# Float32r transposes of the unrounded attention words, released by a one-column POOL memset

## The chip, the cores and the metric

The kernel runs on one core of one Trainium2 chip. The metric is the device time of one execution in microseconds (us), here the median of three runs. The core has five engines that work through their own instruction lists in order: PE (TensorE: matmuls and transposes, with its weight loads shown apart as PEld), DVE (VectorE), ACT (ScalarE), POOL (GpSimd) and SP (which issues the transfers). They wait for one another through semaphores.

## The reference

```python
q_pool = q.reshape(B, H, S // 2, 2, D).mean(axis=3)          # B=2, H=8, S=1152, D=64
scores = (1 / sqrt(D)) * matmul(q_pool, k.transpose(0, 1, 3, 2))
attn = exp(scores - max(scores)); attn = attn / (sum(attn) + 1e-09)
x = matmul(attn, v)                                          # then laid out as [1152, 512]
h = maximum(x @ w_in, 0); x = (s * h * h + b) @ w_out        # d_ff 2048
out = ((x @ w_a) * (x @ w_b)) @ w_out2                       # d_ff 1536
```

All of it is float32. The kernel gets float32 accuracy by splitting operands into a high and a low float32r part (names in h and l) and adding the products.

## The kernel before, in words

Two heads make a pair; there are eight pairs, and each is a **round** of nine **blocks** of 128 pooled query rows by 1152 keys: blocks 0 to 3 are head 0, block 4 holds the rest rows of both heads, and 5 to 8 are head 1. A block g goes through these steps, on the engines named:

- S01 and S2 (L404, L411, PE): scores into PSUM, 768 and 384 columns.
- M01, M2, C (L427, L430, L435, DVE): the row maximum.
- X2, X01 (L439, L446, ACT): exp into the SBUF tile e, with row sums.
- A (L453, POOL, one column): the sum of the row sums; R (L457, DVE): its reciprocal.
- N (L464, POOL, 128x1152): e times the reciprocal, in place. Block 0 of the whole kernel does it in two pieces, columns 512 to 1151 first.
- Ta, Tb, Tc (L481, PE): nine 128x128 transposes of e, of 4, 4 and 1 in three PSUM banks. Here e is the stationary operand, which a weight load brings in, and the identity is what moves through.
- ha to hc (L493, ACT): the high part of each piece out of PSUM; La to Lc (L499, DVE): the low part, which frees the bank.
- PV matmuls (L515, PE) with the tiles p2h, p2l, p3h, p3l.

Beside them POOL splits k and v and pools q for the next pair (kc, v, qp, L95, L98, L325), and splits the attention output (xa_h, xa_l). PE also transposes k (L349, already float32r, three at a time, sharing a bank with Tc) and the pooled q (L369, float32). The order of all steps on every engine is written out by hand in a table, SCHED; nothing is reordered at run time. Three buffers of e go round, four PSUM banks are shared by the transposes, S2 and PV. After attention (about 268 us) come the two MLPs, in which PE does nearly all.

The lines that matter here:

```python
nc.gpsimd.tensor_scalar(out=e[:, c], in0=e[:, c], scalar1=m[:, 6:7], scalar2=1.0, op0=ALU.mult, op1=ALU.mult)  # N
nc.tensor.transpose(ps[:, i * 128:(i + 1) * 128], E[g][:, (c0 + i) * 128:(c0 + i + 1) * 128], ident)           # T
PTC = ((0, 4), (4, 4), (8, 1))                                                                                 # Ta, Tb, Tc
```

Of the kernel before, what the change touches and what calls it, by code (L numbers as in the profile page):

```python
# [9 lines left out]
F32 = mybir.dt.float32  # L10
F32R = mybir.dt.float32r
# [30 lines left out]
def kernel(  # L42
# [14 lines left out]
    nc = tc.nc  # L57
    B, H, S, D = q.shape
# [24 lines left out]
    ident = const.tile([128, 128], F32, name="ident")  # L83
    identr = const.tile([128, 128], F32R, name="identr")
# [171 lines left out]
    att, att_in = ExitStack(), ExitStack()  # L256

    def right(stack, name, bufs, **space):
        return stack.enter_context(tc.tile_pool(name=name, bufs=bufs, side="right", **space))
# [2 lines left out]
    ps_s01 = s01.enter_context(tc.tile_pool(name="ps_s01", bufs=2, space=PSUM))  # L262
    banks = [right(att, f"ps_{i}", 1, space=PSUM) for i in range(4)]
    v_p = right(att, "vv", 2)
    e_p = right(att, "e", 3)
    pt_p = right(att, "pt", 1)
    xs_p = right(att, "xs", 2)
    sm_p = right(att, "sm", 4)
# [13 lines left out]
    def bank(key, reads):  # L282
        held[key] = [free.pop(0), reads]
        return banks[held[key][0]].tile([128, 512], F32, tag="b", name=key[0])
# [7 lines left out]
    KC, X, Q, V, E, RS, SPS = {}, {}, {}, {}, {}, {}, {}  # L292
# [118 lines left out]
            nc.tensor.matmul(ps[:, 0:384], w, x[:, 768:1152], start=(z == 0), stop=(z == len(pr) - 1))  # L411
        SPS[g, 1] = ps

    SM = {}

    def small(g):
        if g not in SM:
            SM[g] = sm_p.tile([128, 8], F32, tag="sm", name="sm")
        return SM[g]

    def e_tile(g):
        if g not in E:
            E[g] = e_p.tile([128, S], F32, tag="e", name="e")
        return E[g]

    def s_max01(g):
# [6 lines left out]
    def s_comb(g):  # L433
        m = SM[g]
        nc.vector.reduce_max(m[:, 2:3], m[:, 0:2], axis=AX.X, negate=True)  # L435

    def s_exp2(g):
        m = SM[g]
        nc.scalar.activation(  # L439
            out=e_tile(g)[:, 768:1152], in_=SPS.pop((g, 1))[:, 0:384], func=AF.Exp, bias=m[:, 2:3], accum_out=m[:, 3:4]  # L440
        )
        bank_read(("s2", g))

    def s_exp01(g):
        m = SM[g]
        nc.scalar.activation(  # L446
            out=e_tile(g)[:, 0:768].rearrange("p (a c) -> p a c", a=2), in_=SPS.pop((g, 0))[:, :, 0:384], func=AF.Exp,
            bias=m[:, 2:3], accum_out=m[:, 4:5],
        )
# [9 lines left out]
    def s_norm(g):  # L459
        m = SM.pop(g)  # L460
        e = E[g]

        for c in (slice(512, S), slice(0, 512)) if g == 0 else (slice(0, S),):
            nc.gpsimd.tensor_scalar(out=e[:, c], in0=e[:, c], scalar1=m[:, 6:7], scalar2=1.0, op0=ALU.mult, op1=ALU.mult)  # L464

    def p_dst(g):
        hd, j = ORDER[g % 9]
        if hd < 2 and j < 2:
            return [t[:, :, j * 128:(j + 1) * 128] for t in p2]
        if hd == 2:  # L470
            return [t[:, :, :, 0:NX] for t in p3]
        c = NX + (j - 2) * 128
        return [t[:, :, hd, c:c + 128] for t in p3]
# [3 lines left out]
    def p_tr(g, z):  # L477
        ps = bank(("t", g, z), 2 + (rides(g) if z == 2 else 0))
        c0, n = PTC[z]
        for i in range(n):  # L480
            nc.tensor.transpose(ps[:, i * 128:(i + 1) * 128], E[g][:, (c0 + i) * 128:(c0 + i + 1) * 128], ident)  # L481
        TP[g, z] = ps

    def p_src(g, z):
# [76 lines left out]
    def rides(g):  # L561
        ahead, reads, _ = RIDES[g % 9]
        return reads if g // 9 + ahead < NP else 0
# [20 lines left out]
    def block(f, *z):  # L584
        return lambda n, i: f(9 * n + i, *z)

    STEPS = dict(
        S01=block(s_mm01), S2=block(s_mm2), M01=block(s_max01), M2=block(s_max2), C=block(s_comb), X2=block(s_exp2),
        X01=block(s_exp01), A=block(s_add), R=block(s_rec), N=block(s_norm), PP=ride,
        EVh=lambda n, i: evac(n, i, 0), EVl=lambda n, i: evac(n, i, 1),  # L590
        KS=then_load(k_split, load_k), QP=then_load(q_pool, load_q), VS=then_load(v_split, load_v),
# [4 lines left out]
    for z, name in enumerate("abc"):  # L596
        STEPS["T" + name], STEPS["h" + name], STEPS["L" + name] = block(p_tr, z), block(p_h, z), block(p_l, z)
# [35 lines left out]
    with tc.manual_schedule():  # L633
# [223 lines left out]
        def pair(i):  # L857
            return ps2[i].tile([128, 2, 512], F32, tag="pp", name="pp")
# [138 lines left out]
        e = pair(0)  # L997
# [62 lines left out]
        ps = [t[:, i] for t in (pair(i) for i in (2, 3, 1, 0)) for i in range(2)]  # L1060
# [55 lines left out]
```

## Time and profile before

| what | us |
|---|---|
| median of three runs | 686.69 (686.60 to 687.19) |
| the profiled execution: its span, first to last instruction | 684.6 |
| median over that span | 2.1 |
| PE busy in the span | 674.3 (98%) |
| DVE, ACT, POOL busy | 521.9, 400.3, 366.6 |
| granted TensorE clock, as share of full speed | 1.00 in every stretch read |

The profile is one execution; its span is the only time it gives for itself, and the median of the unprofiled runs lies 2.1 us above it. Busy shares are means over stages of different kinds. In attention (0 to 268 us) PE, DVE and ACT are all above 90% and POOL at 85%; in the MLPs PE alone is full.

### The profile page before, as it was taken

What the parts mean: (1) busy time and instruction counts of PE and PEld (TensorE: products, weight loads), DVE (VectorE), ACT (ScalarE), POOL (GpSimd) and SP (SyncE); (2) the same over time, 40 slices, a digit from 0 to 9 for tenths busy, and PEclk for the clock granted to TensorE, in tenths of its full rate; (3) what the DMA queues carried; (4) which work ended last, traced back from release to release, by engine and by line L of the source; (5) the groups of instructions that cost most, each with busy time, mean ns of one, the idle gap of its engine ahead of it and who ended that gap; (6) DMA issues with size and microseconds to landing.
All of it is one profiled execution on the core that took longest, in us unless ns stands there. A gap on an engine that the chain in (4) does not pass through costs nothing.

```text
span 684.6 us, 11850 instructions
## 1 busy us (share of the span) xinstructions
PE 674.3 (98%) x4446; PEld 647.0 (95%) x4446; DVE 521.9 (76%) x963; ACT 400.3 (58%) x869; POOL 366.6 (54%) x374
## 2 busy tenths in 40 slices
PE   8999999999999999999999999999999999999997
PEld 7899999999999998999999999999999999998885
DVE  6999999999999996584545744879987888886431
ACT  6998999999999986454531421435433434444321
POOL 5879797979788883586535535510225442430000
PEclk9999999999999999999999999999999999999999
DMA  7121121303030010423223232250132323134004
GB/s 232 38 70 62 44 70 35 82 25 105 2 105 16 20 65 1 152 94 123 63 72 113 63 103 83 64 182 1 62 117 69 125 62 123 62 90 157 0 1 138
DMA packets 25914, 52.93 MB, mean 77 GB/s; under 512 B 1665, under 2 KB 2689, under 8 KB 25857
## 3 DMA queue, kind: packets, MB, share of 16 engines
q1 hardware_dynamic: 25776, 52.04, 23.7%
q8 instruction: 35, 0.57, 0.4%
q14 instruction: 23, 0.18, 0.1%
q10 hardware_dynamic: 80, 0.13, 0.1%
HBM read 49.81 MB, written 2.36 MB: 76 GB/s over the span
## 4 chain that ended last, share of the span: by engine, by line
PE 84%; DVE 9%; ACT 3%; POOL 2%; issue 1%; DMA 1%; SPq 0%; ACTq 0%; POOLq 0%; DVEq 0%
PE ps L630 28%; PE pp L630 17%; PE pp L950 11%; PE pv L515 9%; PE t L481 7%; PE s L404 6%; PE s L411 3%; DVE p3l L499 2%; DVE sm L430 1%; ACT p3h L493 1%; PE t L349 1%; PE t L369 1%; DVE xs L534 1%; DVE sm L427 1%; ACT x L354 1%
## 5 line engine op out<-in xcount | busy, mean ns | idle before, releaser
L481 PE MATMUL t<-ident,e 128*128 128x128 f32 x648 | 98.9, 276 | 2.3 <-POOL e L464 1.0
L464 POOL TENSOR_SCALAR e<-e,sm 128x1152 f32<-128x1152 f32 (+1 forms) x73 | 89.8, 1232 | 10.6 <-DVE sm L457 7.1
L481 PEld LDWEIGHTS t<-ident,e 128*128 128x128 f32 x648 | 75.3, 140 | 12.9 <-POOL e L464 2.3
L965 POOL TENSOR_TENSOR ab<-ab,at 128x576 f32<-128x576 f32 x24 | 35.0, 1478 | 91.0 <-ACT ab L960 87.2
L764 POOL TENSOR_SCALAR r<-r,sb_s,sb_b 128x384 f32<-128x384 f32 (+1 forms) x46 | 41.0, 902 | 57.7 <-DVE r L761 57.7
L499 DVE TENSOR_TENSOR p3l<-t,p3h 128x512 fp32r<-128x512 f32 (+1 forms) x120 | 64.2, 554 | 6.6 <-ACT p3h L493 4.2
L427 DVE TENSOR_REDUCE sm<-s 128x1 f32<-128x768 f32 x72 | 68.2, 948 | 0.1
L446 ACT ACTIVATE e<-s,sm 128x768 f32<-128x768 f32 x72 | 66.5, 923 | 0.4 <-DVE sm L435 0.4
L493 ACT CAST p3h<-t 128x512 fp32r<-128x512 f32 (+1 forms) x120 | 56.2, 485 | 5.1 <-PE t L481 2.7
L758 ACT ACTIVATE r<-ps 128x384 f32<-128x384 f32 (+1 forms) x46 | 20.1, 505 | 61.8 <-PE ps L630 61.7
L761 DVE SCALAR_TENSOR_TENSOR r<-ps,r 128x384 f32<-128x384 f32 (+1 forms) x46 | 23.8, 567 | 37.2 <-ACT r L758 37.2
L499 DVE TENSOR_TENSOR p2l<-t,p2h 128x512 fp32r<-128x512 f32 x96 | 50.8, 549 | 0.9 <-ACT p2h L493 0.7
L142 ACT ACTIVATE f<-raw 128x1024 f32<-128x1024 f32 x34 | 38.8, 1140 | 17.9 <-issue 11.1
L515 PE MATMUL pv<-p3h,v 128*128 128x320 f32 x144 | 47.6, 338 | 0.4 <-DVE p2l L499 0.4
L493 ACT CAST p2h<-t 128x512 fp32r<-128x512 f32 x96 | 45.0, 501 | 5.1 <-PE t L481 4.3
L439 ACT ACTIVATE e<-s,sm 128x384 f32<-128x384 f32 x72 | 43.0, 597 | 5.8 <-DVE sm L457 4.7
L630 PE MATMUL ps<-xa_h,wh 128*128 128x384 f32 (+1 forms) x200 | 45.3, 330 | 0.1
L146 DVE SCALAR_TENSOR_TENSOR f<-raw,f 128x1024 int32<-128x1024 int32 x34 | 44.5, 1309 | 1.1
L630 PE MATMUL ps<-xa_h,wl 128*128 128x384 f32 (+1 forms) x200 | 45.0, 328 | 0.0
L630 PE MATMUL ps<-xa_l,wh 128*128 128x384 f32 (+1 forms) x200 | 45.0, 328 | 0.0
L166 POOL TENSOR_TENSOR wl<-f,wh 128x1024 fp32r<-128x1024 f32 x16 | 40.5, 2531 | 7.1 <-ACT wh L198 5.9
L630 PE MATMUL ps<-gh,wh 128*128 128x384 f32 x192 | 43.7, 336 | 0.0
(142 smaller groups left out, 2047.1 us busy)
## 6 DMA issues: line engine op xcount, KB each, us to landing
raw<-in_moe_w_out_dram SPq DMA_DIRECT2D x14, 1024.0 KB, 5.0
raw<-in_moe_w_in_dram SPq DMA_DIRECT2D x8, 1024.0 KB, 5.7
raw<-in_moe_w_a_dram SPq DMA_DIRECT2D x6, 1024.0 KB, 5.2
raw<-in_moe_w_b_dram SPq DMA_DIRECT2D x6, 1024.0 KB, 5.1
vn<-in_v_dram SPq DMA_DIRECT2D x8, 576.0 KB, 4.0
kn<-in_k_dram SPq DMA_DIRECT2D x7, 576.0 KB, 3.9
qn<-in_q_dram SPq DMA_DIRECT2D x7, 512.0 KB, 3.8
out_dram<-ab SPq DMA_DIRECT2D x8, 256.0 KB, 2.6
```

The costliest lines, as they stand in the source:

```text
L146: nc.vector.scalar_tensor_tensor(out=f, in0=lo, scalar=29, in1=f, op0=ALU.logical_shift_right, op1=ALU.bitwise_or)
L404: nc.tensor.matmul(ps[:, c, 0:384], w, x[:, c * 384:(c + 1) * 384], start=(z == 0), stop=(z == len(pr) - 1))
L427: nc.vector.reduce_max(small(g)[:, 0:1], SPS[g, 0][:, :, 0:384], axis=AX.XY)
L439: nc.scalar.activation(out=e_tile(g)[:, 768:1152], in_=SPS.pop((g, 1))[:, 0:384], func=AF.Exp, bias=m[:, 2:3], accum_out=m[:, 3:4])
L446: nc.scalar.activation(out=e_tile(g)[:, 0:768].rearrange("p (a c) -> p a c", a=2), in_=SPS.pop((g, 0))[:, :, 0:384], func=AF.Exp, bias=m[: ...
L464: nc.gpsimd.tensor_scalar(out=e[:, c], in0=e[:, c], scalar1=m[:, 6:7], scalar2=1.0, op0=ALU.mult, op1=ALU.mult)
L481: nc.tensor.transpose(ps[:, i * 128:(i + 1) * 128], E[g][:, (c0 + i) * 128:(c0 + i + 1) * 128], ident)
L493: nc.scalar.copy(out=p_dst(g)[0][:, c0:c0 + n], in_=p_src(g, z))
L499: nc.vector.tensor_tensor(out=l, in0=p_src(g, z), in1=h.bitcast(F32), op=ALU.subtract)
L515: nc.tensor.matmul(ps[:, 0:N], V[n, hd][:, c].rearrange("p a d -> p (a d)"), p, start=(t == 0), stop=(t == 2 * NC - 1))
L630: nc.tensor.matmul(ps, a, c[:, o:o + n], start=(first and z == 0), stop=(last and z == 2), skip_group_check=more)
L950: nc.tensor.matmul(ps, a[x], w2_at[kf][c], start=(kf == 0 and y == 0), stop=(kf == KF2 - 1 and y == 2))
```

## The change

The transposes of Ta, Tb and Tc become float32r. A tile er of type float32r is laid over the same place as e (three pools of one buffer each in place of one pool of three), one spare group of eight columns wider. The words in it are those that N wrote as float32, unrounded. Since nothing writes er as far as the scheduler can see, N is followed by a POOL memset of one spare column of er, and each transpose is made to depend on that memset. The identity is the float32r one, and the result goes to PSUM under a float32r view.

```diff
-    e_p = right(att, "e", 3)
+    e_ps = [right(att, f"e{i}", 1) for i in range(3)]
...
-            E[g] = e_p.tile([128, S], F32, tag="e", name="e")
+            E[g] = e_ps[g % 3].tile([128, S + 8], F32, tag="e", name="e")[:, 0:S]
...
         for c in (slice(512, S), slice(0, 512)) if g == 0 else (slice(0, S),):
             nc.gpsimd.tensor_scalar(out=e[:, c], in0=e[:, c], scalar1=m[:, 6:7], scalar2=1.0, op0=ALU.mult, op1=ALU.mult)
+        er = e_ps[g % 3].tile([128, S + 8], F32R, tag="e", name="er")
+        ER[g] = er, nc.gpsimd.memset(er[:, S:S + 1].bitcast(F32), 0.0)
...
+        er, ready = ER[g]
         for i in range(n):
-            nc.tensor.transpose(ps[:, i * 128:(i + 1) * 128], E[g][:, (c0 + i) * 128:(c0 + i + 1) * 128], ident)
+            t = nc.tensor.transpose(ps[:, i * 128:(i + 1) * 128].bitcast(F32R), er[:, (c0 + i) * 128:(c0 + i + 1) * 128], identr)
+            tc.add_manual_dep(
+                t.ins, ready.ins.name, mybir.DependencyInfo(mybir.DependencyClass.Sync, mybir.DependencyReason.DATA),
+                reason="the words of e",
+            )
```

On POOL, the stretch of a round from A of block 3 to N of block 6 stood like this (sm is the tile of row sums, e that of a block; "waits Pool" is a wait of POOL for its own earlier instruction to complete):

```order
L453 TENSOR_SCALAR sm<-sm 128x1 [waits Activation_49]
L95 TENSOR_SCALAR kc<-kn 128x9x64 [waits DMAHW2_49,PE_49]
L98 TENSOR_TENSOR kc<-kn,kc 128x9x64 [waits Pool_49]
L464 TENSOR_SCALAR e<-e,sm 128x1152 [waits DVE_49]
L325 TENSOR_TENSOR qp<-qn 128x512 [waits DMAHW7_49,PE_49]
L453 TENSOR_SCALAR sm<-sm 128x1 [waits Activation_49]
L95 TENSOR_SCALAR v<-vn 128x9x64 [waits PE_49]
L98 TENSOR_TENSOR v<-vn,v 128x9x64 [waits Pool_49]
L464 TENSOR_SCALAR e<-e,sm 128x1152 [waits DVE_49]
L453 TENSOR_SCALAR sm<-sm 128x1 [waits Activation_49]
```

The same stretch on POOL with the change:

```order
L453 TENSOR_SCALAR sm<-sm 128x1 [waits Activation_49]
L95 TENSOR_SCALAR kc<-kn 128x9x64 [waits DMAHW2_49,PE_49]
L98 TENSOR_TENSOR kc<-kn,kc 128x9x64 [waits Pool_49]
L464 TENSOR_SCALAR e<-e,sm 128x1152 [waits DVE_49]
L466 MEMSET er 128x1 [waits Pool_49]
L325 TENSOR_TENSOR qp<-qn 128x512 [waits DMAHW7_49,PE_49]
L453 TENSOR_SCALAR sm<-sm 128x1 [waits Activation_49]
L95 TENSOR_SCALAR v<-vn 128x9x64 [waits PE_49]
L98 TENSOR_TENSOR v<-vn,v 128x9x64 [waits Pool_49]
L464 TENSOR_SCALAR e<-e,sm 128x1152 [waits DVE_49]
L466 MEMSET er 128x1 [waits Pool_49]
L453 TENSOR_SCALAR sm<-sm 128x1 [waits Activation_49]
```

Nothing else moved on POOL: each N has a memset behind it that waits for that N to complete, 72 in all, and what followed N now follows the memset.

On PE, the first block's transposes (Tb, the scores of block 3, Ta and Tc, then transposes of k) stood like this:

```order
L481 MATMUL t<-ident,e 128x128 [waits Activation_49,Pool_49]
L481 MATMUL t<-ident,e 128x128 x3
L404 MATMUL s_295<-x,qh 128x384 [waits Activation_49]
L404 MATMUL s_295<-x,qh 128x384
L404 MATMUL s_295<-x,ql 128x384 x2
L481 MATMUL t<-ident,e 128x128 [waits Pool_49]
L481 MATMUL t<-ident,e 128x128 x3
L481 MATMUL t<-ident,e 128x128 [waits PE_49]
```

With the change the same place on PE reads:

```order
L484 MATMUL t<-identr,er 128x128 [waits Activation_49,Pool_49]
L484 MATMUL t<-identr,er 128x128 x3
L404 MATMUL s_303<-x,qh 128x384 [waits Activation_49]
L404 MATMUL s_303<-x,qh 128x384
L404 MATMUL s_303<-x,ql 128x384 x2
L484 MATMUL t<-identr,er 128x128 x4
L484 MATMUL t<-identr,er 128x128 [waits PE_49]
```

The second wait for POOL is gone here, since the first one is now for the memset, which stands behind both pieces of the first block's N. Elsewhere the order on PE, ACT and DVE is the same as before.

## Rows read from the trace of the kernel before

**Rows 1.** Busy time by engine in two of six whole rounds, and their mean.
```profile
core 0: us, PE busy (x) PEld busy (x) DVE busy (x) ACT busy (x) POOL busy (x), PEclk, DMA share, GB/s
67.58:99.93 32.35, 32.24 (x243) 31.04 (x242) 30.77 (x73) 29.81 (x78) 27.39 (x34) 1.00 0.20 54
99.93:132.28 32.35, 32.24 (x243) 31.05 (x242) 30.78 (x73) 29.82 (x78) 27.38 (x34) 1.00 0.20 58
...
sum 194.18, PE 193.40 PEld 185.96 DVE 185.19 ACT 180.04 POOL 164.33; mean PE 32.23 PEld 30.99 DVE 30.86 ACT 30.01 POOL 27.39
```

**Rows 2.** Chain of work that ended last, pieces at 99 us: start, length, what.
```profile
99.41 1.11 PE t L481 x9
100.52 0.33 PE t L369 x3
...
104.62 0.21 PE t L349 x3
```

**Rows 3.** Weight loads of six float32r transposes in a row, early: start, length.
```profile
5.86 0.59 PEld L349 LDWEIGHTS t<-identr,kc 128*128 128x128 f32 x6
```

**Rows 4.** POOL in time from block 2's N on; [idle before <- what ended it].
```profile
113.88 1.23 POOL L464 TENSOR_SCALAR e<-e,sm 128x1152 f32<-128x1152 f32 x1
115.33 0.29 POOL L453 TENSOR_SCALAR sm<-sm 128x1 f32<-128x1 f32 x1 [0.22 <-ACT e L446]
115.70 0.67 POOL L95 TENSOR_SCALAR kc<-kn 128x576 fp32r<-128x576 f32 x1
116.46 1.43 POOL L98 TENSOR_TENSOR kc<-kn,kc 128x576 fp32r<-128x576 f32 x1
117.87 1.22 POOL L464 TENSOR_SCALAR e<-e,sm 128x1152 f32<-128x1152 f32 x1
119.07 1.30 POOL L325 TENSOR_TENSOR qp<-qn 128x512 f32<-128x512 f32 x1
120.47 0.29 POOL L453 TENSOR_SCALAR sm<-sm 128x1 f32<-128x1 f32 x1
...
126.24 0.29 POOL L453 TENSOR_SCALAR sm<-sm 128x1 f32<-128x1 f32 x1
126.63 2.44 POOL L464 TENSOR_SCALAR e<-e,sm 128x1152 f32<-128x1152 f32 x2
```

**Rows 5.** Weight loads around block 5's transposes.
```profile
127.52 0.36 PEld L404 LDWEIGHTS s<-x,ql 128*128 128x128 f32 x2
127.92 0.64 PEld L481 LDWEIGHTS t<-ident,e 128*128 128x128 f32 x5
```

**Rows 6.** POOL's N of block 8, then its first transpose's weight load.
```profile
105.30 1.23 POOL L464 TENSOR_SCALAR e<-e,sm 128x1152 f32<-128x1152 f32 x1
...
106.60 0.14 PEld L481 LDWEIGHTS t<-ident,e 128*128 128x128 f32 x1
```

**Rows 7.** ACT in time: where it waits for PE, and two exps.
```profile
107.22 0.48 ACT L354 CAST x<-t 128x384 fp32r<-128x384 f32 x1 [0.34 <-PE t L349]
...
114.16 0.98 ACT L446 ACTIVATE e<-s,sm 128x768 f32<-128x768 f32 x1
...
128.68 0.59 ACT L493 CAST p2h<-t 128x512 fp32r<-128x512 f32 x1
...
132.34 1.08 ACT L493 CAST p2h<-t 128x512 fp32r<-128x512 f32 x2 [0.40 <-PE t L481]
...
133.93 0.96 ACT L446 ACTIVATE e<-s,sm 128x768 f32<-128x768 f32 x1
```

**Rows 8.** DVE behind block 5's transposes: its low parts.
```profile
129.34 0.68 DVE L499 TENSOR_TENSOR p2l<-t,p2h 128x512 fp32r<-128x512 f32 x1
...
131.25 0.87 DVE L499 TENSOR_TENSOR p2l<-t,p2h 128x128 fp32r<-128x128 f32 x2
```

**Rows 9.** POOL's one-column memsets at the start of the program.
```profile
0.24 0.10 POOL L1100 MEMSET const-float32-0.0<- 128x1 f32 x1 [0.24 <-issue]
0.27 0.10 POOL L1100 MEMSET const-float32-1.0<- 128x1 f32 x1
```

**Rows 10.** Chain that ended last at the first block and at block 4.
```profile
12.78 0.81 POOL e L464
13.59 0.04 issue
13.63 0.67 PE t L481 x4
...
24.61 0.30 POOL sm L453
```

**Rows 11.** The first block's N on POOL, and what follows it.
```profile
12.78 1.46 POOL L464 TENSOR_SCALAR e<-e,sm 128x640 f32<-128x640 f32 x2 [0.30 <-DVE sm L457]
14.35 0.29 POOL L453 TENSOR_SCALAR sm<-sm 128x1 f32<-128x1 f32 x1
```

**Rows 12.** Groups of the whole span: transposes and their weight loads.
```profile
L481 PE MATMUL t<-ident,e 128*128 128x128 f32 x648 | 98.9, 276 | 2.3 <-POOL e L464 1.0
...
L481 PEld LDWEIGHTS t<-ident,e 128*128 128x128 f32 x648 | 75.3, 140 | 12.9 <-POOL e L464 2.3
```

More of the change, by code (lines that the diff above doesn't have):

```diff
@@ L412, in s_mm2 @@
         SPS[g, 1] = ps
-    SM = {}
+    SM, ER = {}, {}
     def small(g):
```

## The prediction

> **What bounds the kernel now.** I first read the busy times of six whole rounds (32.35 us each) [rows 1]: PE 32.23 of 32.35, DVE 30.86, ACT 30.01, POOL 27.39. PE looks like the bound, and the change takes work from PE. But DVE has only 1.5 us of idle time in a round, so even a free PE could shorten a round by no more than that. Next I read the chain that ended last; in the middle of a round it is mostly PE, transposes included [rows 2]. A chain names one path and says nothing of paths that are nearly as long. So I followed POOL, the engine that gets the new instructions, in time, and asked where PE takes up what POOL has just finished. There are two such places in every round, and at both there is no slack:
>
> - Block 5. POOL waits for the exp of block 3 (0.22 us of idle, ended by ACT) and starts its A at 115.33. From there to the end of block 5's N at 127.86 it runs without waiting; no gap is longer than 0.11 us [rows 4]. The next weight load on PE that needs this N starts at 127.92, 0.06 us later, which is the time a semaphore takes [rows 5]. A load starts as a rule when the matmul before it starts, which was 127.87, so this one already came 0.05 us late, and its matmul at 128.04 had some 0.02 us to spare.
> - Block 8. N runs from 105.30 to 106.53, and the weight load starts at 106.60 [rows 6].
>
> Between them a round can be cut into four legs, which add up to 32.35:
> 1. Block 8's transposes (106.70) to the end of block 3's exp (115.14, [rows 7]): 8.44. ACT waits 0.34 for transposes at 107.22 and then not again until that exp.
> 2. 115.14 to block 5's transposes (128.04): 12.90, POOL's run above.
> 3. 128.04 to the end of block 8's exp (134.89): 6.85, through ACT and DVE, which take up block 5's transposes at 128.68 and 129.34 [rows 7, 8], and through block 6's transposes, for which ACT waits 0.40 at 132.34.
> 4. 134.89 to the next block 8's transposes (106.70 + 32.35 = 139.05): 4.16, again on POOL (A, the split of v, N).
>
> **What the transposes save.** The nine float32 transposes of a block take 1.11 in the chain and three of q 0.33, or 0.11 to 0.12 each; three float32r transposes of k take 0.21, or 0.07 each [rows 2]. Six float32r in a row have their weight loads within 0.59; less the 0.14 of one load [rows 12] that is 0.45 for five steps, 0.09 each [rows 3]. So a transpose gets cheaper by 0.02 to 0.04. I take 0.03, between the long and the short runs, since Ta, Tb and Tc are runs of 1, 4 and 5: 81 x 0.03 = 2.4 us of PE a round. The mean of 276 ns [rows 12] is no price, since 648 of them are 98.9 us of union only because they overlap their neighbours.
>
> The Trainium skill (TensorE: Matmul & The Clock Gate, Part 4: PE-mode transpose) gives about 275 ns for a transpose in a kernel and lays most of it to access latency, so the type would not matter. The record's 276 ns agrees as a length, the steps of 0.11 against 0.07 speak against it as a cost; by that rule the saving is nothing, which is the third rival below.
>
> **What the memset costs.** Of its kind there are four one-column memsets of 0.10, started 0.03 apart without waits [rows 9]. The new ones wait for their N. Such a wait shows between the two steps of kc: 115.70 + 0.67 = 116.37, and the next starts at 116.46, 0.09 (0.08 before rounding) [rows 4]. Before the change the instruction behind N starts with or before N's end (117.87 + 1.22 = 119.09 against 119.07). So 0.08 + 0.10 = 0.18 us for POOL, and for PE's release too. Below: 0.08 + 0.03 = 0.11, if only the spacing counts. Above: the other one-column instruction, A, takes 0.29 with 0.08 behind it (115.33 to 115.70), with the wait 0.45 [rows 4]. I take 0.18: the same operation and size, while A is a different operation.
>
> [...]
>
> **The sum of a round**, at 0.18 a memset:
> - Leg 2. A of block 3 now follows block 2's memset: N ends at 115.11, plus 0.18, plus the 0.10 that A shows behind a long instruction (119.07 + 1.30 to 120.47, [rows 4]), is 115.39 against 115.33, so +0.06. Three memsets (blocks 3, 4, 5) +0.54. Spare -0.02. Leg: +0.58. Whatever PE saves between 115 and 128 is waited away here: PE arrives earlier and waits for the memset of block 5. Behind it in PE's order stand the rest of that block's transposes, q's, PV and scores, which ACT and DVE then lack.
> - Leg 3. The four transposes of a bank end three steps of 0.04 earlier, 0.12, once at block 5 and once at block 6; PE's work between saves some more, but block 6's bank is freed by DVE (the second low part, 131.25), which is itself behind block 5. -0.32, between -0.24 by DVE and -0.44 by PE.
> - Leg 4. One memset, +0.18, spare -0.04: +0.14.
> - Leg 1. ACT runs on from k's transposes, which move with block 8's: 0.
>
> Together +0.40 a round. Block 5's transposes at 128.04 stand three rounds behind 31.0 and three ahead of 225.1, six rounds: **+2.4 us**.
>
> **The start.** The first block's N is in two pieces, and Tb was released by the first, at 13.63 [rows 10]. Now it waits for a memset behind both: 12.78 + 1.46 = 14.24 [rows 11], + 0.18 + 0.05 = 14.47, so 0.84 later. Its four transposes give 0.12 back: +0.7 on a stretch where the chain goes from that transpose straight into ACT. Up to block 4's A (24.61, [rows 10]) another memset stands on POOL's path: +0.2. Together **+0.9**.
>
> **The end**, from 225 us on: the last seven blocks have 63 transposes; I count some 50 of them on PE's path, which gives back 50 x 0.03 = 1.5 us, and ten memsets on POOL's path to the last transposes, 1.8 us: **+0.3**. The MLPs only shift.
>
> Sum 2.4 + 0.9 + 0.3 = +3.6 on a span of 684.6: 688.2. The median lay 2.1 above the span, so I forecast **690.3 us** against 686.69, 0.5% slower. With memsets at 0.11 leg 2 is +0.31 (0 + 3 x 0.11 - 0.02), leg 4 +0.07, a round +0.06: 0.4 + 0.8 - 0.1 = +1.1, 687.8. At 0.45 leg 2 is +1.67, leg 4 +0.41, a round +1.76: 10.6 + 1.7 + 1.4 = +13.7, 700.4; I hold that unlikely, and the range stops short of it.
>
> **Rivals.**
> - *Faster: POOL's run is not what holds PE.* If PE, ACT and DVE have other work at block 5 whose order doesn't hang on it, the freed PE time shows until DVE is full: of 1.5 us of idle some 0.4 are gaps under 0.1 us that stay, so -1.1 a round, -6.6, and +0.7 at the start: about 681. For it: DVE's idle time in a round lies mostly before block 5. Against it: that load starts 0.06 us behind N [rows 5], and ACT and DVE take up block 5 at once [rows 7, 8]. It decides if the memset costs leg 2 less than legs 3 and 4 give back, below about 0.10. Chance 0.2.
> - *No change: the memset hides at the spacing of 0.03.* Leg 2 +0.07, leg 4 0, leg 3 -0.32: -0.25 a round, -1.5, start +0.7, end -0.3: 685.6. Against it: it waits for N, and such waits cost 0.08. With the lower bound above, chance 0.2.
> - *Slower still: float32r transposes cost the same.* Leg 3 and the start's return vanish: +0.58 + 0.18 = +0.76 a round, 4.6, start +1.0, end +1.8: 694.1. Against it the 0.07 of k's transposes. Chance 0.05.
> - *My forecast*, memsets between 0.12 and 0.45: 0.55.
>
> A measurement here tells some 0.2% (1.4 us) from no change. Faster 0.2, same 0.2, slower 0.6. The range is 683 to 694: below it lies most of the first rival's full size, above it the memset near its upper bound, each about a tenth. Given the forecast case its own range is 688.2 to 694.
>
> **What would show it right or wrong.** In the profile after: transposes in short runs 0.07 to 0.09 apart; a MEMSET of about 0.10 behind each N, starting 0.08 after it; POOL's run from block 3's A to block 5's memset near 13.1 instead of 12.5; at block 5 and 8 PE idle and waiting for POOL's memset, some 1 us at block 5; rounds of 32.6 to 32.9 instead of 32.35; Tb of the first block at about 14.5. I am wrong if rounds are shorter than 32.35, if PE stays full, or if ACT and DVE keep working through PE's wait at block 5.

## The result, and the profile after

| | before | after |
|---|---|---|
| median of 4 runs each, same chip (us) | 686.64 (686.40 to 687.19) | 694.33 (693.56 to 694.40) |
| span of the profiled execution | 684.6 | 691.8 |

The change makes the kernel slower: the ratio is 1.0107, 95% interval 1.0095 to 1.0119. The forecast was 690.3, range 683 to 694; the direction was right, the size was not (+7.7 us instead of +3.6), and the time lies 0.33 us above the range. The profiled execution is the changed kernel's shortest, 693.56 us; the other three took 694.27 to 694.40, so the span's +7.2 is less than the median's +7.7.

Two whole rounds in a row of the profile after, in the columns of [rows 1]:

```profile
65.01:98.34 33.33, 31.36 (x240) 29.58 (x240) 30.59 (x74) 29.83 (x78) 28.40 (x43) 1.00 0.18 55
98.34:131.62 33.28, 31.35 (x240) 29.53 (x240) 30.58 (x74) 29.83 (x78) 28.35 (x43) 1.00 0.20 55
```

A round takes 33.31 us instead of 32.34 (the sums of the legs measured below; rounds given later without a row are means over middle rounds, measured in the same way). PE's work fell by 0.9 us, so the transposes did get cheaper; POOL's rose by 1.0 (it was 85% of a round before; of the whole of attention, 0 to 268 us, it was 81%); and PE, which was busy in all but 0.1 us of a round, now stands idle for some 1.95.

The groups of the whole span (busy us, mean ns of one | idle before them, and what ended it):

```profile
L484 PE MATMUL t<-identr,er 128*128 128x128 f32 x648 | 79.8, 245 | 15.8 <-POOL er L466 8.1 <-DVE p2l L506 3.3 <-DVE sm L435 2.4
...
L457 DVE RECIPROCAL sm<-sm 128x1 f32<-128x1 f32 x72 | 11.5, 160 | 12.5 <-POOL sm L453 12.0
...
L466 POOL MEMSET er<- 128x1 f32 x72 | 7.1, 99 | 4.3
```

The memset itself takes 99 ns, and POOL's idle time ahead of the 72 is 4.3 us, 0.06 each: it starts 0.06 behind its N. Idle time ahead of the transposes rose from 2.3 us [rows 12] to 15.8.

The waits of the whole span (engine, its line <- what it waited for: us in total, times, longest us):

```profile
POOL sm L453 <- ACT e L446: 14.1, 18, 1.6
...
PEld t L484 <- POOL er L466: 13.2, 18, 1.8
...
DVE sm L457 <- POOL sm L453: 12.0, 25, 0.8
ACT p2h L500 <- PE t L484: 11.9, 17, 1.1
...
PE t L484 <- POOL er L466: 8.1, 14, 1.4
```

All the lower four are waits for POOL, or for a PE that waited for POOL; in the same view of the kernel before, the second stood at 2.3 us, the third at 1.9 and the fourth at 4.3. The first one, POOL's own wait for ACT, fell from 20.4. So POOL waits less for others, and the others wait for POOL. The third wait (R, on DVE, for A) is one that the prediction does not mention.

The chain that ended last, shares of the span by engine; before, PE had 84% of it and POOL 2%:

```profile
PE 63%; POOL 15%; DVE 10%; ACT 8%; issue 3%; POOLq 0%; ACTq 0%; DVEq 0%
```

POOL in time, over one round's run (start, length, instruction, [idle <- what ended it]):

```profile
118.31 0.10 POOL L466 MEMSET er<- 128x1 f32 x1
118.52 0.29 POOL L453 TENSOR_SCALAR sm<-sm 128x1 f32<-128x1 f32 x1
...
121.06 1.24 POOL L464 TENSOR_SCALAR e<-e,sm 128x1152 f32<-128x1152 f32 x1
122.36 0.10 POOL L466 MEMSET er<- 128x1 f32 x1
122.46 1.29 POOL L325 TENSOR_TENSOR qp<-qn 128x512 f32<-128x512 f32 x1
...
130.19 1.23 POOL L464 TENSOR_SCALAR e<-e,sm 128x1152 f32<-128x1152 f32 x1
131.47 0.10 POOL L466 MEMSET er<- 128x1 f32 x1
131.60 1.23 POOL L464 TENSOR_SCALAR e<-e,sm 128x1152 f32<-128x1152 f32 x1
132.89 0.10 POOL L466 MEMSET er<- 128x1 f32 x1
132.94 1.30 POOL L325 TENSOR_TENSOR qp<-qn 128x512 f32<-128x512 f32 x1
134.19 0.47 POOL L325 TENSOR_TENSOR qpm<-qm 128x128 f32<-128x128 f32 x1
134.77 0.29 POOL L453 TENSOR_SCALAR sm<-sm 128x1 f32<-128x1 f32 x1
135.43 1.24 POOL L464 TENSOR_SCALAR e<-e,sm 128x1152 f32<-128x1152 f32 x1 [0.36 <-PE s L404]
136.73 0.10 POOL L466 MEMSET er<- 128x1 f32 x1
136.79 0.68 POOL L95 TENSOR_SCALAR kc<-kn 128x576 fp32r<-128x576 f32 x1
137.55 1.44 POOL L98 TENSOR_TENSOR kc<-kn,kc 128x576 fp32r<-128x576 f32 x1
139.10 0.29 POOL L453 TENSOR_SCALAR sm<-sm 128x1 f32<-128x1 f32 x1
...
142.94 0.10 POOL L466 MEMSET er<- 128x1 f32 x1
```

From block 3's A (118.52) to the end of block 8's memset (143.04) POOL has one idle time over 0.11 us, the 0.36 before block 7's N, and that is only the time of R between A and N (the profile names PE there; before, it puts the same 0.37 down to R, in the rows below). So the run did not end at block 5, as the prediction took it: it goes on through block 8 and holds six memsets (blocks 3 to 8). It takes 24.52 us. Before, it took 23.52: from 115.33 [rows 4] to the end of block 8's N, 137.62 + 1.23 = 138.85. The difference, 1.00, is the whole growth of a round, 0.97, within 0.03. What lies outside the run is 8.82 of a round before and 8.79 after.

And before, that run had nearly no slack either. These are rows of the kernel before that the prediction did not read, POOL at blocks 7 and 8:

```profile
131.50 1.23 POOL L464 TENSOR_SCALAR e<-e,sm 128x1152 f32<-128x1152 f32 x1 [0.37 <-DVE sm L457]
...
133.45 1.43 POOL L98 TENSOR_TENSOR kc<-kn,kc 128x576 fp32r<-128x576 f32 x1
135.09 0.29 POOL L453 TENSOR_SCALAR sm<-sm 128x1 f32<-128x1 f32 x1 [0.20 <-ACT e L446]
...
137.62 1.23 POOL L464 TENSOR_SCALAR e<-e,sm 128x1152 f32<-128x1152 f32 x1
```

A of block 8 waits 0.20 for ACT's exp, but as A starts 0.10 behind a long instruction without any wait [rows 4], ACT cost POOL only 0.10 us.

How the lateness spreads beyond block 5 is seen on DVE, where two waits for POOL's A (block 6's, then block 7's) stand ahead of the low parts that free the transposes' banks:

```profile
130.12 0.16 DVE L457 RECIPROCAL sm<-sm 128x1 f32<-128x1 f32 x1 [0.64 <-POOL sm L453]
...
135.10 0.16 DVE L457 RECIPROCAL sm<-sm 128x1 f32<-128x1 f32 x1 [0.44 <-POOL sm L453]
135.18 0.87 DVE L506 TENSOR_TENSOR p2l<-t,p2h 128x128 fp32r<-128x128 f32 x2
```

PE's transposes of block 6 wait for that low part:

```profile
135.59 0.93 PE L484 MATMUL t<-identr,er 128*128 128x128 f32 x9 [0.32 <-DVE p2l L506]
```

ACT waits for those transposes, and block 8's exp, which ends at 138.69, stands behind:

```profile
136.14 0.59 ACT L500 CAST p2h<-t 128x512 fp32r<-128x512 f32 x1 [0.70 <-PE t L484]
...
137.73 0.96 ACT L446 ACTIVATE e<-s,sm 128x768 f32<-128x768 f32 x1
```

PE's weight loads stand idle for 1.17 us ahead of block 5's transposes, and for 0.48 ahead of block 8's:

```profile
131.62 0.48 PEld L484 LDWEIGHTS t<-identr,er 128*128 128x128 f32 x5 [1.17 <-POOL er L466]
...
143.09 0.14 PEld L484 LDWEIGHTS t<-identr,er 128*128 128x128 f32 x1 [0.48 <-POOL er L466]
```

The prediction's four legs of a round, measured alike in both traces from the starts of the weight loads and the ends of the exps:

| leg | before | after | moved | predicted |
|---|---|---|---|---|
| 1: block 8's transposes to block 3's exp | 8.54 | 8.49 | -0.05 | 0 |
| 2: to block 5's transposes | 12.77 | 13.36 | +0.59 | +0.58 |
| 3: to the end of block 8's exp | 6.97 | 7.07 | +0.10 | -0.32 |
| 4: to block 8's transposes | 4.06 | 4.40 | +0.34 | +0.14 |
| round | 32.34 | 33.31 | +0.97 | +0.40 |

### The profile page after: what moved, and what is told of

It reads as the page before. It is cut to its first block, busy times and chain, and to the rows that moved or that the text cites. A ratio compares the mean times of both kernels' runs of the same rounds, so it can differ in the third digit from the quotient of the medians.

```text
span 691.8 us, 11922 instructions
## 1 busy us (share of the span) xinstructions
PE 667.6 (97%) x4446; PEld 636.0 (92%) x4446; DVE 520.9 (75%) x963; ACT 399.8 (58%) x869; POOL 374.8 (54%) x446
## 4 chain that ended last, share of the span: by engine, by line
PE 63%; POOL 15%; DVE 10%; ACT 8%; issue 3%; POOLq 0%; ACTq 0%; DVEq 0%
PE ps L637 28%; PE pp L637 17%; PE pp L957 11%; POOL e L464 5%; DVE p3l L506 3%; POOL v L98 2%; PE t L484 2%; ACT e L446 2%; ACT p2h L500 2%; PE pv L522 2%; PE s L404 2%; POOL sm L453 2%; POOL kc L98 2%; ACT p3h L500 1%; POOL v L95 1%
## 5 line engine op out<-in xcount | busy, mean ns | idle before, releaser
L484 PE MATMUL t<-identr,er 128*128 128x128 f32 x648 | 79.8, 245 | 15.8 <-POOL er L466 8.1
L484 PEld LDWEIGHTS t<-identr,er 128*128 128x128 f32 x648 | 67.3, 140 | 29.0 <-POOL er L466 13.2
```

The source lines that it names most:

```text
L484: t = nc.tensor.transpose(ps[:, i * 128:(i + 1) * 128].bitcast(F32R), er[:, (c0 + i) * 128:(c0 + i + 1) * 128], identr)
```

## The experiments

Two theories stand against each other in the expectations. **P**: POOL's run from block 3's A through block 8's memset sets the round, and what a transpose costs hardly matters beside it. **R**: the accounting on record, with the transposes' saving given back in legs 3 and 4. Each comparison is with the kernel before on the same chip; its median was 686.56 us beside the first four kernels, 686.18 beside the next four and 686.47 beside the last two.

**The memset alone.** The tile over e's place is float32, the transposes are those of before, and the memset, the dependency and the three pools stay.

```diff
-        er = e_ps[g % 3].tile([128, S + 8], F32R, tag="e", name="er")
+        er = e_ps[g % 3].tile([128, S + 8], F32, tag="e", name="er")
...
-            t = nc.tensor.transpose(ps[:, i * 128:(i + 1) * 128].bitcast(F32R), er[:, (c0 + i) * 128:(c0 + i + 1) * 128], identr)
+            t = nc.tensor.transpose(ps[:, i * 128:(i + 1) * 128], er[:, (c0 + i) * 128:(c0 + i + 1) * 128], ident)
```

> Float32 transposes as before, but with the memset behind each N and the transposes waiting for it. Theory P (POOL's run from block 3's A through to block 8's memset, six memsets long, sets the round; the price of a transpose hardly matters): 694 to 696 us, as the changed kernel or 1 us above it. Theory R (the accounting on record: memsets of blocks 3, 4, 5 and 8 count, and cheaper transposes give 0.3 to 0.4 us a round back): with that return gone, about 697 us. If the memset is not the cause at all: 687.

Measured: 695.16 us, ratio 1.0118 (1.0101 to 1.0135). One round of it:

```profile
99.67:132.99 33.32, 32.65 (x240) 30.99 (x240) 30.90 (x74) 29.84 (x80) 28.38 (x43) 1.00 0.18 55
```

The round is that of the changed kernel, 33.32, with PE's work 1.3 us higher. The memset, with the wait for it and the split pools that come with it, makes the whole loss, and the cheaper transposes give a round nothing back beside it. By R this kernel would have stood near 697, above the change by what the transposes give back; the two ratios' intervals overlap. The split of the pools was not run alone; the only wait on er that the profile after lists outside PE is 0.3 us of ACT in the whole span.

**The float32r transposes alone.** From the kernel before: the exps and N round e to float32r and no memset is needed; the low part of P then is nearly zero, with the same instructions.

```diff
-            E[g] = e_p.tile([128, S], F32, tag="e", name="e")
+            E[g] = e_p.tile([128, S], F32R, tag="e", name="e")
...
-            nc.tensor.transpose(ps[:, i * 128:(i + 1) * 128], E[g][:, (c0 + i) * 128:(c0 + i + 1) * 128], ident)
+            nc.tensor.transpose(ps[:, i * 128:(i + 1) * 128].bitcast(F32R), E[g][:, (c0 + i) * 128:(c0 + i + 1) * 128], identr)
```

> Float32r transposes without any memset: the exps and N write e rounded to float32r, so the low part of P is nearly zero; everything else is as before. Theory P: POOL's run is as long as before and had no slack, so rounds stay within 0.2 us of 32.35: 685 to 687 us. Theory R: 0.3 to 0.4 us a round and more at the end come back: 682 to 684. If PE were the bound: about 680.

Measured: 685.31 us, ratio 0.9986 (0.9976 to 0.9995). One round:

```profile
95.50:127.80 32.30, 31.34 (x241) 29.57 (x241) 30.64 (x74) 29.91 (x80) 27.52 (x34) 1.00 0.20 56
```

PE is relieved of 0.9 us a round and the round gets 0.07 shorter (32.27 in the mean). That is what P allows: POOL's run had only 0.10 of slack to give.

**No memset for blocks 6 and 7.** In the changed kernel the exps and N of these two blocks round e to float32r, and the transposes wait for N. R has no cost for these two memsets, P has.

```diff
-            E[g] = e_ps[g % 3].tile([128, S + 8], F32, tag="e", name="e")[:, 0:S]
+            E[g] = e_ps[g % 3].tile([128, S + 8], F32R if g % 9 in (6, 7) else F32, tag="e", name="e")[:, 0:S]
...
+        if g % 9 in (6, 7):
+            ER[g] = e, nm
+            return
```

> The changed kernel without the memsets of blocks 6 and 7 of each round (their exps and N round to float32r in place; the low part of P is nearly zero there). Theory P: these two stand in POOL's run ahead of A of blocks 7 and 8, so a round gets 0.3 to 0.35 us shorter: 691.5 to 692.5 us. Theory R: neither stands ahead of block 5's or block 8's transposes where POOL is late, so nothing changes: 694.3.

Measured: 692.19 us, ratio 1.0082 (1.0067 to 1.0097); the round is 33.02. POOL in time at the same place:

```profile
131.12 1.23 POOL L464 TENSOR_SCALAR e<-e,sm 128x1152 fp32r<-128x1152 f32 x1
132.32 1.29 POOL L325 TENSOR_TENSOR qp<-qn 128x512 f32<-128x512 f32 x1
```

What follows N starts 1.20 after N's start, where the changed kernel has 1.34 (131.60 to 132.94). The two memsets are worth 0.29 a round (0.30 to 0.35 was expected) and 2.1 us of the time. R gave 694.3 and falls; this run tells the two apart.

**A on ACT.** The changed kernel with A moved from POOL to ACT (the 1e-9 is left out of the sum there).

```diff
-        nc.gpsimd.tensor_scalar(out=m[:, 5:6], in0=m[:, 3:4], scalar1=1e-9, scalar2=m[:, 4:5], op0=ALU.add, op1=ALU.add)
+        nc.scalar.activation(out=m[:, 5:6], in_=m[:, 3:4], func=AF.Identity, bias=m[:, 4:5])
```

> The changed kernel with A (the sum of the two row sums) on ACT in place of POOL, so that POOL's run loses 0.37 to 0.40 us at each of the blocks 4 to 8. Theory P: 1.5 to 1.9 us a round less on POOL's run, until DVE (30.8 us busy) or ACT (30 us and nine more instructions of about 0.2) holds the round: 684 to 689 us. Theory R: blocks 4, 5 and 8 count, 1.1 us a round, less what ACT loses: 687 to 690. If POOL is not the bound in the changed kernel: 695 or more, since ACT gets more work.

Measured: 693.72 us, ratio 1.0104 (1.0089 to 1.0119), not the 684 to 689 that P gave. One round, and the moved A over the whole span:

```profile
98.17:131.13 32.96, 31.94 (x241) 29.64 (x240) 30.54 (x73) 31.66 (x89) 25.73 (x34) 1.00 0.21 55
```

```profile
L453 ACT ACTIVATE sm<-sm 128x1 f32<-128x1 f32 x72 | 22.4, 311 | 0.8
```

PE's weight loads wait for POOL's memset for 4.3 us instead of 13.2, so POOL was relieved, and the round is 0.35 shorter than with the change. But A takes 0.31 us on ACT, where 0.2 was expected, ACT is now busy for 31.66 of 32.96, and R on DVE waits for A on ACT for 6.5 us in all. That ACT has taken POOL's place is read from these numbers; no run shows it.

**A left out.** So A was taken away instead: R takes the reciprocal of the row sum over 768 of the 1152 columns, and the rows are scaled by that. This was done to the changed kernel (first), to the kernel before (second), and to the one with float32r transposes alone (third).

```diff
-        nc.gpsimd.tensor_scalar(out=m[:, 5:6], in0=m[:, 3:4], scalar1=1e-9, scalar2=m[:, 4:5], op0=ALU.add, op1=ALU.add)
+        return
...
-        nc.vector.reciprocal(m[:, 6:7], m[:, 5:6])
+        nc.vector.reciprocal(m[:, 6:7], m[:, 4:5])
```

> The changed kernel without A: the reciprocal is taken of the sum over 768 of the 1152 columns, so the rows are scaled wrongly; no other engine gets work in its place. Theory P (POOL's run holds the rounds of the changed kernel): that run loses 0.37 us at each of six blocks, rounds of 31.2 to 32.0 in place of 33.3, held by DVE: 679 to 685 us, below the kernel before. If POOL only looks late because another engine is: 693 to 694.

> The kernel before without A in the same way. Theory P: before the change PE is full (32.2 of 32.35) and POOL only just in time, so a lighter POOL gives little: rounds of 32.2 to 32.35, 685 to 687 us. If POOL already held the rounds before: 680 or less.

> Float32r transposes without memset (exps and N round to float32r in place, the low part of P is nearly zero) and without A as in the two others. Theory P: with POOL out of the way the cheaper transposes at last shorten the round, to the 31.2 us or so that DVE needs: 677 to 681 us, 5 us or more below the same with float32 transposes. If transposes are not worth anything: as that one, 685 to 687.

| A left out of | us | ratio (95%) |
|---|---|---|
| the changed kernel | 680.64 | 0.9921 (0.9906 to 0.9936) |
| the kernel before | 685.26 | 0.9987 (0.9978 to 0.9997) |
| float32r transposes alone | 678.72 | 0.9894 (0.9879 to 0.9909) |

One round of the first:

```profile
94.60:125.90 31.30, 30.84 (x241) 29.61 (x240) 30.35 (x73) 29.77 (x80) 25.77 (x34) 1.00 0.20 58
```

of the second:

```profile
94.70:126.91 32.21, 32.13 (x242) 31.06 (x241) 30.75 (x73) 29.78 (x80) 24.78 (x25) 1.00 0.19 56
```

and of the third:

```profile
93.08:124.40 31.32, 30.85 (x242) 29.72 (x241) 30.37 (x73) 29.74 (x80) 24.84 (x25) 1.00 0.20 58
```

With float32 transposes, taking 2.6 us of POOL's work away shortens a round by 0.13: PE is then full (32.13 of 32.21). With float32r transposes as well it is 31.3, and there the memsets cost a round nothing (31.30 with them, 31.32 without). In the whole time they are 1.92 us apart (680.64 and 678.72). So before the change PE and POOL's run were bounds of nearly the same length, each within 0.13 us of the round. Relieving one alone gives 0.07 (the transposes alone) or 0.13 (A left out), relieving both gives 1.0. In the whole time the float32r transposes are worth 6.5 us without A (685.26 to 678.72) and 1.25 with it (686.56 to 685.31).

Leaving A out does two things, though: it takes work from POOL, and it takes an instruction and a wait out of the path from the exps to N. With A on ACT, left out, or on DVE (next), POOL's work in a round is the same, 25.73, 25.77 and 25.66, and the rounds are 32.96, 31.30 and 32.45. So POOL's work alone does not give these rounds; the engine that takes A over, or the length of that path, counts too, and no run separates the two.

**A on DVE.** The same but complete: A moves to DVE, right ahead of R.

```diff
-        nc.gpsimd.tensor_scalar(out=m[:, 5:6], in0=m[:, 3:4], scalar1=1e-9, scalar2=m[:, 4:5], op0=ALU.add, op1=ALU.add)
+        return
...
+        nc.vector.tensor_scalar(out=m[:, 5:6], in0=m[:, 3:4], scalar1=1e-9, scalar2=m[:, 4:5], op0=ALU.add, op1=ALU.add)
         nc.vector.reciprocal(m[:, 6:7], m[:, 5:6])
```

> The changed kernel, complete, with A on DVE right ahead of the reciprocal. POOL's run loses 0.37 us a block, DVE gains nine instructions of 0.1 to 0.15 us a round on 30.8 us. Theory P: rounds near what DVE then needs, 32.2 to 32.6: 685 to 689 us. If DVE has no room at all: 692 or more.

Measured: 690.21 us, ratio 1.0055 (1.0038 to 1.0072). One round, and A on DVE over the whole span:

```profile
98.90:131.35 32.45, 31.58 (x241) 29.52 (x240) 31.57 (x82) 29.84 (x79) 25.66 (x34) 1.00 0.19 56
```

```profile
L457 DVE TENSOR_SCALAR sm<-sm 128x1 f32<-128x1 f32 x72 | 14.7, 204 | 0.4
```

The round is 0.86 shorter than with the change, as expected. DVE, with 0.20 for each A, is full up to 0.9 us of it. The time missed the expected range because of the start: the first weight load of block 5's transposes comes at 34.03, against 31.70 with the change and 30.94 before. The first block's transposes stand at 14.16, where the change has 14.21, so all of the 2.3 us over the change arises behind them. There the granted TensorE clock fell from 1.00 to 0.50, the lower of its two levels (1.2 GHz of 2.4), twice, each time soon after PE had waited:

```profile
14.16 0.54 PE L485 MATMUL t<-identr,er 128*128 128x128 f32 x4 [1.44 <-POOL er L467]
...
24.69 0.50 PE L485 MATMUL t<-identr,er 128*128 128x128 f32 x4 [0.59 <-DVE p3l L507]
```

```profile
15.00:18.00 3.00, 3.00 (x18) 2.81 (x16) 1.95 (x3) 2.92 (x8) 0.63 (x2) 0.50 0.44 168
25.50:28.50 3.00, 3.00 (x15) 3.00 (x14) 2.10 (x7) 2.08 (x6) 2.92 (x3) 0.50 0.00 0
```

In the profile of the changed kernel PE waits 1.45 for the same memset, and both stretches stand at 1.00. An execution of the kernel with A on DVE whose clock was 1.000 over the whole took 688.97 us, inside the expected range.

**A in part on DVE, and on DVE and ACT.** Then A was moved to DVE for blocks 4, 5 and 7 only (first), and besides to ACT for blocks 6 and 8 (second; the 1e-9 is left out in those).

```diff
+        if g % 9 in (4, 5, 7):
+            return
+        if g % 9 in (6, 8):
+            nc.scalar.activation(out=m[:, 5:6], in_=m[:, 3:4], func=AF.Identity, bias=m[:, 4:5])
+            return
...
+        if g % 9 in (4, 5, 7):
+            nc.vector.tensor_scalar(out=m[:, 5:6], in0=m[:, 3:4], scalar1=1e-9, scalar2=m[:, 4:5], op0=ALU.add, op1=ALU.add)
```

> The changed kernel, complete, with A of blocks 4, 5 and 7 of a round on DVE, the others on POOL. Theory P: POOL's run loses 3 x 0.37 = 1.1 us, a round of about 32.2 in place of 33.3, DVE stays under that (about 31): 686 to 688 us. If the gain goes only to blocks 4 and 5: 689.

> The same, and A of blocks 6 and 8 on ACT. Theory P: POOL's run loses five A's, 1.85 us; DVE and ACT have about 31 and 30.5 us a round, so some 31.7 to 32.1: 682 to 686 us, which would be under the kernel before. If A on ACT costs there what it did with all nine, 688 or more.

Measured: 688.62 us, ratio 1.0034 (1.0021 to 1.0046), and 688.50, ratio 1.0030 (1.0020 to 1.0040); both miss what was expected. The round of the first is 32.42 in the mean, against about 32.2 expected. One round of the second:

```profile
98.00:130.26 32.26, 31.45 (x243) 29.61 (x241) 30.98 (x76) 30.26 (x81) 26.80 (x38) 1.00 0.21 56
```

Its rounds are now shorter than those of the kernel before (32.26 against 32.34), but not by the 0.2 to 0.6 expected, and the start costs 1.7 us: block 5's first weight load stands at 32.66 instead of 30.94. Against the change that is 0.96 later, and here too the granted clock was at 0.50, from 15.0 to 18.0. No complete version that transposes the unrounded words was found that beats the kernel before. Why a round with A spread like this stays 0.96 above that without A is not settled. A division in N in place of R, and another order of POOL's work, were not tried.

## Why the prediction was right or wrong

**Right.** The memset's price: 0.10 and 0.06 of waiting, 0.14 to 0.20 between what stands around it, against the 0.18 taken. The Trainium skill (Perfetto Trace Analysis, GPSIMD Engine Instruction) advises to time POOL's instructions by the spacing of their starts, not by their spans. Here that matters little: N to the pooling of q went from 1.20 [rows 4] to 1.40 (121.06 to 122.46), and from N to N it is 1.41. The transposes' price: five weight loads of block 5 within 0.48 instead of 0.64 [rows 5]; less the 0.14 of one, and over four steps, 0.085 instead of 0.125, so 0.04 where 0.03 was taken. Leg 1, and leg 2 with PE's wait at block 5 (1.17, "some 1 us"). The start: block 5's first weight load is 0.76 later, against 0.9, in part by luck: the execution profiled began its first N 0.25 earlier than the one before (12.53 against 12.78), so the first transposes stood at 14.21 and not near 14.5. The forecast has no term for a fall of the clock behind them, which the profiles of all seven experiments with that memset show.

**Wrong: leg 3, "-0.32, between -0.24 by DVE and -0.44 by PE".** It measured +0.10, off by 0.42 a round and 2.5 us over six. The step was costed along PE, ACT and DVE, as if POOL, once block 5 had its N, had time in hand until block 8. It had 0.10. So the memsets of blocks 6 and 7 were put at nothing, without a reason; the run without them shows their cost, 0.29 a round. And the -0.32 that the transposes were to give back did not come: with float32 transposes beside the memset the round is the same, 33.32. The row that says how little slack there was, A of block 8 with 0.20 of idle, was in the trace and was not read. Block 6's memset, like those before it, pushes A of block 7, which holds R on DVE, the low parts behind R, the bank, block 6's transposes, and ACT; block 7's pushes kc and with it A of block 8.

**Wrong: leg 4, "+0.14".** It measured +0.34, 1.2 us over six rounds. It took block 8's A as released by the exp. Now it is released by POOL's own kc: it starts 0.41 behind the exp's end (139.10 against 138.69), where before it was 0.20 (135.09 against 134.89). That adds 0.21. From that A to the weight load it is 3.99 instead of 3.86 (the leg less these waits), so the memset itself added 0.13, as forecast.

Worked out again, an estimate from these rows: six memsets at 0.18 less the 0.10 of slack are +0.98 a round, measured +0.97, and no term for the transposes. Over six rounds the trace shows +5.8 where +2.4 was forecast, the start +0.8 for 0.9; block 8's transposes of the last pair come another 0.7 later than that (+7.3 in all), with +0.3 forecast for the end. How the end's part is made up was not tested.

The forecast's bounds have a slip of their own: at the end, ten memsets less the 1.5 us given back come to -0.4, +3.0 and -1.2 at 0.11, 0.45 and 0.03 a memset, where -0.1, +1.4 and -0.3 are added. It moves the lower bound to 687.5 and the second rival to 684.7, and decides nothing here.

**The rivals.** That the freed PE time shows (681) and that the memset hides (685.6) both fell. The third, that float32r transposes cost the same, gave 694.1, nearly the time measured, for a reason that is wrong: they do cost less, and without A that is worth 6.5 us. The Trainium skill (TensorE: Matmul & The Clock Gate, Part 4: PE-mode transpose) gives some 275 ns for a transpose in a kernel and lays most of it to access latency. It gives no figure by type there; that the type would not matter was the prediction's inference, and these runs speak against it. The type doesn't matter only where PE waits for POOL anyway.

## What to carry to other kernels

An engine with in-order work is followed through the whole period, from one wait that it does not cause to the next, and its run is cut off only where its idle time exceeds what it shows behind any instruction; a wait of 0.20 in front of an instruction is not 0.20 of slack. POOL had the least busy time of the four engines in a round (28.4 of 33.3 us), and its run still set how much the round grew. The Trainium skill (Perfetto Trace Analysis, Identifying the Most-Contended Engine) would have one work first on the engine with the highest occupancy, TensorE judged by its weight loads. That was PE here (PEld 30.99, DVE 30.86 a round, [rows 1]), and relieving PE alone gave 0.07 us a round until POOL was relieved too. Where two runs of different engines are equally long, price an edit on each apart and take the longer sum, for what the shorter one saves is waited away.

## What the runs showed that was not expected

- The one-column addition A took 0.30 us on POOL (72 take 21.3 us), 0.31 on ACT and 0.20 on DVE, where about 0.2 and 0.1 to 0.15 had been expected for the last two; a one-column memset on POOL takes 0.10.
- The memset started 0.06 us behind the N that it waits for; the wait between the two steps of kc, taken as the model, shows 0.08.
- With float32r transposes and A left out, a round falls to 31.3 us with PE busy for 30.84 and POOL for 25.8; what ends it there was not looked into.
- PE's wait for the first block's memset (1.1 to 1.5 us, where the kernels without one show 0.37 to 0.67) was followed, in the profiles of all seven experiments that have that memset, by a granted clock of 0.50 for some 3 us, between 14 and 19 us. In the profile of the changed kernel, with 1.45 of waiting, the clock stayed at 1.00, as it did there in the kernels without the memset. What makes it fall in one execution and not in another was not looked into.
